# Threshold attention into a bilinear FFN: the scores of the last 64 queries on the other two 64x64 tiles of the PE array

## The chip, the cores and the metric

The kernel runs on one core of a Trainium2 chip. The metric is the device time of one execution in microseconds (us): 1541.02 us before the change, the median of three runs (1540.39 to 1543.94). Profiles are of one execution each.

## The reference, cut to what matters

There are 8 batches of 8 heads, 576 positions and head size 64, everything in fp32. The 64 heads' outputs are laid side by side per batch into 4608 rows of 512, which go through a bilinear feed-forward network (FFN) with 1536 inner columns.

```python
scores = scale * np.matmul(q, k.transpose(0, 1, 3, 2))
thresh = np.max(scores, axis=-1, keepdims=True) - tau
scores = np.where(scores >= thresh, scores, -1000000000.0)
scores = scores - np.max(scores, axis=-1, keepdims=True)
attn = np.exp(scores)
attn = attn / (np.sum(attn, axis=-1, keepdims=True) + 1e-09)
attn_out = np.matmul(attn, v)                      # (8, 8, 576, 64)
x = attn_out.transpose(0, 2, 1, 3).reshape(4608, 512)
out = (x @ w_a) * (x @ w_b) @ w_out
```

## The kernel before, in words

**Tiles of the array.** Every large product is cut to 64 contraction rows by 64 output columns, so each matmul occupies one quarter of the 128x128 PE array. Which quarter follows from the partitions: the operands' partitions (0-63 or 64-127) give the row half r, the output's partitions give the column half c. This text writes a tile as (r,c). (0,0) and (1,1) are the diagonal pair, (0,1) and (1,0) the off-diagonal pair. Both halves of a head pair lie in the two partition halves of `qT` and `kT`, so r is the head in a pair.

**Units.** The 64 heads are 32 pairs. A pair's 576 queries are five units: `u` = 0 to 3 with 128 queries each and `u` = 4 (`NT`) with the last 64 (`TAIL`). `scores` (L303 to L322) multiplies a unit's queries with all 576 keys in two halves `c` of 288. A full unit has eight matmuls, two on each tile, into two buffers of the accumulation memory (PSUM), one a head. The last unit has four, all into one buffer: head 0 into its lower 64 partitions, head 1 into its upper 64.

**After the scores.** DVE takes each row's maximum (L319), GpSimd the threshold and the bias (L320, L321), ACT the exponential (L332), DVE masks and sums (L336), ACT divides (L355). `turn_blocks` (L393 to L426) has DVE transpose 32x32 blocks into `tb` (for the last unit, `tbt`), sends them out to a scratch tensor `swap` in DRAM, from where `turn_back` fetches the transposed weights `wT` for two parts of a pair: 256 queries (units 0 and 1), and 320 (units 2, 3 and 4). For the first four pairs the parts are 256, 256 and 64 wide, and their first eight units are turned on the PE instead.

**Product with v.** `product` (L441 to L451) multiplies a part's `wT` with `v`. The 1152 keys of a pair (576 a head) are nine slots of 128 partitions: four for each head, which use all four tiles in turn, and slot `NT`, which the heads share: its lower 64 partitions hold keys of head 0 and its upper 64 keys of head 1. In that slot there are only two matmuls, (0,0) and (1,1). It comes first in the product.

**FFN.** `ffn` (L505 to L563) is a generator of small steps; each step on `pab` (L530, the products with `w_a` and `w_b`, 256 columns) and on `po` (L550, the product with `w_out`, 512 columns) issues four matmuls, in the order (0,0), (0,1), (1,0), (1,1). A block of 256 rows is 2 x 6 groups of `pab` with 8 steps, and 2 groups of `po` with 12.

**Order.** The loop from L634 writes the order of all engines' instructions out by hand, and `keep_order` keeps it. One turn `g` issues the scores of unit `g`, then FFN steps (`advance`, in portions), the weighing of unit `g`, more FFN steps, the product of a part whose last unit was four turns ago (`PV_LAG`, L675 to L679), and FFN steps. After the first four pairs, a group of four pairs takes 20 turns (L616, L617):

```python
units += [(p, u) for p in range(i, i + HP) for u in (0, 1)]
units += [(p, u) for p in range(i, i + HP) for u in (2, 3, NT)]
```

With the turns of a group counted from 0, its last units have their scores in turns 10, 13, 16 and 19, its products of 256 come in turns 5, 7, 9 and 11, and those of 320 in turns 14, 17, 20 and 23 (the last two are turns 0 and 3 of the next group).

Of the kernel before, what the change touches and what calls it, by code (L numbers as in the profile page):

```python
# [50 lines left out]
def kernel(  # L51
# [8 lines left out]
    w_out: bass.AP,  # L60
    out: bass.AP,
):

# [23 lines left out]
    B, H, S, D = q.shape  # L89
    P = 128  # L90
# [4 lines left out]
    NT = 4  # L95
    MAIN = NT * P
    TAIL = S - MAIN
    assert D == 64 and TAIL == 64 and DM == HP * P
    NB = S // Q
# [22 lines left out]
    def banks(n, name):  # L122

        return psum.tile([P, 2, 512], FP32, tag="banks", name=name)[:, :, 0:n]
# [120 lines left out]
    for _ in range(2):  # L245
        t = work.tile([P, 2 * NB, 2 * Q], FP32, tag="tb", bufs=2, name="rows")
        t = t.rearrange("p n e -> p (n e)")[0:R]
# [11 lines left out]
    for name in ("q", "k"):  # L259
        t = work.tile([P, CW, 2], FP32, tag="xT", bufs=XT_BUFS, name="rows")  # L260
        t = t.rearrange("p n e -> p (n e)")[0:R, 0:2 * NR * D]
# [41 lines left out]
    def scores(i, u):  # L303
        qT, kT = prepared[i]["q"], prepared[i]["k"]
        n = 2 if u < NT else 1
        sc = [banks(SH, "sc") for _ in range(n)]
        for c in range(2):
            for t in range(n):
                for j in range(2):
                    r = slice(j * D, (j + 1) * D)  # L310
                    q0, to = (u * P + t * D, slice(t * D, (t + 1) * D)) if u < NT else (MAIN, r)
                    nc.tensor.matmul(sc[j if u < NT else 0][to, c], qT[r, q0:q0 + D],  # L312
                                     kT[r, c * SH:(c + 1) * SH], start=True, stop=True)
        mx = small.tile([P, 2], FP32, tag="mx", name="mx")
        thr = small.tile([P, 2], FP32, tag="thr", name="thr")
        bias = small.tile([P, 2], FP32, tag="bias", name="bias")
        for j in range(n):
            c = slice(j, j + 1)
            nc.vector.tensor_reduce(mx[:, c], sc[j], axis=AX.XY, op=ALU.max)  # L319
            nc.gpsimd.tensor_scalar(bias[:, c], mx[:, c], e_nscale, None, op0=ALU.mult)  # L320
        nc.gpsimd.tensor_scalar(thr[:, 0:n], mx[:, 0:n], cut, None, op0=ALU.subtract)  # L321
        scored[i, u] = (sc, thr, bias)  # L322
# [61 lines left out]
    def part(i, u):  # L384

        if i < HP:
            return {1: (i, 0), 3: (i, 1), NT: (i, 2)}.get(u)
        return {1: (i, 0), NT: (i, 1)}.get(u)

    def width(i, h):  # L390
        return (HALF, HALF, TAIL)[h] if i < HP else (HALF, HALF + TAIL)[h]

    def turn_blocks(i, u):  # L393

        ws, _ = weights.pop((i, u))
        if u < NT:
            if u % 2 == 0:
                tbufs[i] = work.tile([P, 2 * NB, 2 * Q], FP32, tag="tb", bufs=2, name="tb")
            tb = tbufs[i]
            for j, w in enumerate(ws):  # L400
                nc.vector.transpose(  # L401
                    tb[:, j * NB:(j + 1) * NB, (u % 2) * Q:(u % 2 + 1) * Q],
                    w.rearrange("p (n e) -> p n e", e=Q))
            if u % 2 == 0:
                return
            h = u // 2
            n = width(i, h)
            swap = scratch.tile([2 * NB, Q, n], FP32, tag=f"swap{n}", name="swap")
            swaps[i, h] = swap
            for g in range(G):  # L410
                nc.sync.dma_start(  # L411
                    swap[:, :, g * 2 * Q:(g + 1) * 2 * Q].rearrange("c p w -> p c w"),
                    tb[g * Q:(g + 1) * Q])
        else:
            tb = work.tile([P, S], FP32, tag="w", bufs=W_BUFS, name="tbt").rearrange("p (n e) -> p n e", e=Q)
            nc.vector.transpose(tb.rearrange("p n e -> p (n e)"), ws[0])
            if i < HP:
                swaps[i, 2] = scratch.tile([2 * NB, Q, TAIL], FP32, tag="swapt", name="swap")
            swap = swaps[part(i, u)]
            for g in range(G):  # L420
                c = slice(g // 2 * NB, (g // 2 + 1) * NB)
                w0 = swap.shape[2] - TAIL + (g % 2) * Q
                nc.sync.dma_start(swap[c, :, w0:w0 + Q].rearrange("c p w -> p c w"),  # L423
                                  tb[g * Q:(g + 1) * Q])
        if part(i, u):
            ready.append(part(i, u))  # L426
# [207 lines left out]
    for g in range(len(units) + PV_LAG):  # L634
# [3 lines left out]
        if here:  # L638
            i, u = units[g]
            scores(i, u)  # L640
# [18 lines left out]
        if g > BY_PE and g <= len(units):  # L659
            turn_blocks(*units[g - 1])  # L660
# [86 lines left out]
```

## Time and profile before

| what | value |
|---|---|
| time | 1541.02 us (1540.39 to 1543.94) |
| PE matmuls (PE) | busy 1484.0 us, 96%, 22640 records |
| PE weight loads (PEld) | busy 1145.4 us, 74% |
| DVE / ACT / GpSimd | busy 878.4 / 590.0 / 261.6 us, 57 / 38 / 17% |
| records of the scores (L312) | 2304 |
| records of the product with v (L449) | 2592 |
| DMA queue q1 | 64.1% of sixteen engines' span |

The kernel's code has 1152 score matmuls (128 full units of eight, 32 last units of four); the profile has 2304 records on their line, two for each. So one fp32 matmul is two passes of its tile, each with its own weight load and record. Records of the same pass on different tiles overlap, and the busy time of a row counts overlapped time once: a row's busy time says little about how many of the four tiles ran. A record's length is modelled, and longer than the tile is occupied. The spacing of the starts on one tile tells that.

### The profile page before, as it was taken

What the parts mean: (1) busy time and instruction counts of PE and PEld (TensorE: products, weight loads), DVE (VectorE), ACT (ScalarE), POOL (GpSimd) and SP (SyncE); (2) the same over time, 40 slices, a digit from 0 to 9 for tenths busy, and PEclk for the clock granted to TensorE, in tenths of its full rate; (3) what the DMA queues carried; (4) which work ended last, traced back from release to release, by engine and by line L of the source; (5) the groups of instructions that cost most, each with busy time, mean ns of one, the idle gap of its engine ahead of it and who ended that gap; (6) DMA issues with size and microseconds to landing.
All of it is one profiled execution on the core that took longest, in us unless ns stands there. A gap on an engine that the chain in (4) does not pass through costs nothing.

```text
span 1541.0 us, 51117 instructions
## 1 busy us (share of the span) xinstructions
PE 1484.0 (96%) x22640; PEld 1145.4 (74%) x22640; DVE 878.4 (57%) x1844; ACT 590.0 (38%) x935; POOL 261.6 (17%) x662
## 2 busy tenths in 40 slices
PE   5778999999999999999999999999999999999998
PEld 3666786675777576778777787877777879798886
DVE  5999676567656765665545754576645665510010
ACT  4767354334433443443323433344433443410000
POOL 2666211101110111020100101011110111110000
PEclk8889999999999999999999999999999999999999
DMA  9658888679868876795547966588748876430000
GB/s 202 150 139 226 173 174 194 163 152 188 192 148 155 185 182 150 147 193 133 123 100 145 190 149 138 119 173 177 171 95 159 182 173 125 123 84 15 2 15 15
DMA packets 624557, 220.38 MB, mean 143 GB/s; under 512 B 542928, under 2 KB 612048, under 8 KB 624336
## 3 DMA queue, kind: packets, MB, share of 16 engines
q1 hardware_dynamic: 621968, 216.52, 64.1%
q8 instruction: 178, 2.92, 0.8%
q10 hardware_dynamic: 2368, 0.59, 0.2%
q14 instruction: 43, 0.35, 0.1%
HBM read 127.40 MB, written 89.65 MB: 141 GB/s over the span
## 4 chain that ended last, share of the span: by engine, by line
PE 88%; DVE 5%; SPq 2%; ACT 1%; issue 1%; DMA 1%; POOL 0%; POOLq 0%; DVEq 0%; ACTq 0%
PE pab L530 45%; PE po L550 24%; PE pv L449 9%; PE sc L312 9%; DVE low L226 1%; SPq L140 1%; DVE w L336 1%; DVE mx L319 1%; SPq L411 1%; DMA raw<-in_moe_w_b_dram 0%; PE tp L374 0%; DVE tb L401 0%; SPq L423 0%; DVE wb_sb L232 0%; DVE wo_sb L232 0%
## 5 line engine op out<-in xcount | busy, mean ns | idle before, releaser
L550 PE MATMUL po<-wo_sb,h 64*64 64x512 f32 x3456 | 424.3, 589 | 0.0
L550 PEld LDWEIGHTS po<-wo_sb,h 64*64 64x64 f32 x3456 | 222.8, 133 | 137.6 <-issue 79.7
L319 DVE TENSOR_REDUCE mx<-sc 128x1 f32<-128x576 f32 x288 | 205.0, 748 | 201.4 <-PE sc L312 201.2
L332 ACT ACTIVATE w<-sc,bias,scalars 128x576 f32<-128x576 f32 x288 | 226.8, 827 | 190.2 <-POOL bias L320 178.7
L312 PE MATMUL sc<-kT,qT 64*64 64x288 f32 x2304 | 264.1, 412 | 21.5 <-DVE w L336 9.8
L530 PE MATMUL pab<-xS,wa_sb 64*64 64x256 f32 (+1 forms) x3520 | 278.7, 376 | 3.3 <-POOL xS L459 3.3
L530 PE MATMUL pab<-xS,wb_sb 64*64 64x256 f32 (+1 forms) x3520 | 279.4, 377 | 2.5 <-issue 2.5
L355 ACT ACTIVATE w<-w,rcp 128x576 f32<-128x576 f32 x272 | 197.7, 768 | 182.9 <-DVE rcp L349 182.7
L320 POOL TENSOR_SCALAR bias<-mx,scalars 128x1 f32<-128x1 f32 x288 | 85.5, 297 | 1050.3 <-DVE mx L319 624.5
L530 PE MATMUL pab<-xT,wb_sb 64*64 64x256 f32 (+1 forms) x3136 | 250.9, 377 | 0.5 <-DVE h L538 0.5
L530 PE MATMUL pab<-xT,wa_sb 64*64 64x256 f32 (+1 forms) x3136 | 243.4, 373 | 4.4 <-DVE xT L439 3.5
L336 DVE SCALAR_TENSOR_TENSOR w<-sc,thr,w 128x576 f32<-128x576 f32 x288 | 222.4, 804 | 20.5 <-ACT w L332 17.8
L530 PEld LDWEIGHTS pab<-xS,wa_sb 64*64 64x64 f32 x3520 | 193.4, 134 | 33.6 <-POOL xS L459 9.8
L530 PEld LDWEIGHTS pab<-xS,wb_sb 64*64 64x64 f32 x3520 | 196.5, 135 | 27.9 <-issue 3.1
L312 PEld LDWEIGHTS sc<-kT,qT 64*64 64x64 f32 x2304 | 148.2, 134 | 71.6 <-issue 18.3
L530 PEld LDWEIGHTS pab<-xT,wa_sb 64*64 64x64 f32 x3136 | 170.4, 133 | 30.4 <-DVE xT L439 3.8
L530 PEld LDWEIGHTS pab<-xT,wb_sb 64*64 64x64 f32 x3136 | 173.5, 135 | 24.4 <-DVE h L538 1.1
L449 PE MATMUL pv<-wT,vm 64*64 64x320 f32 (+3 forms) x2592 | 186.1, 382 | 1.9 <-ACT h L536 1.4
L401 DVE STREAM_TRANSPOSE tb<-w 128x576 f32<-128x576 f32 x240 | 171.3, 752 | 1.3 <-ACT w L355 1.3
L449 PEld LDWEIGHTS pv<-wT,vm 64*64 64x64 f32 x2592 | 138.8, 134 | 37.3 <-issue 7.4
L538 DVE TENSOR_TENSOR h<-h,pab 128x512 f32<-128x512 f32 (+1 forms) x110 | 72.8, 662 | 125.3 <-PE pab L530 124.8
L536 ACT COPY h<-pab 128x512 f32<-128x512 f32 (+1 forms) x110 | 63.2, 574 | 203.9 <-PE pab L530 203.1
(59 smaller groups left out, 747.9 us busy)
## 6 DMA issues: line engine op xcount, KB each, us to landing
swap<-tb SPq DMA_DIRECT2D x240, 288.0 KB, 5.3
wT<-swap SPq DMA_DIRECT2D x28, 1440.0 KB, 7.4
wT<-swap SPq DMA_DIRECT2D x32, 1152.0 KB, 6.4
vm<-in_v_dram SPq DMA_DIRECT2D x32, 288.0 KB, 4.5
swap<-tbt SPq DMA_DIRECT2D x128, 72.0 KB, 2.6
out_dram<-osb SPq DMA_DIRECT2D x32, 256.0 KB, 4.0
qm<-in_q_dram SPq DMA_DIRECT2D x112, 72.0 KB, 3.5
km<-in_k_dram SPq DMA_DIRECT2D x112, 72.0 KB, 4.4
```

The costliest lines, as they stand in the source:

```text
L312: nc.tensor.matmul(sc[j if u < NT else 0][to, c], qT[r, q0:q0 + D], kT[r, c * SH:(c + 1) * SH], start=True, stop=True)
L319: nc.vector.tensor_reduce(mx[:, c], sc[j], axis=AX.XY, op=ALU.max)
L320: nc.gpsimd.tensor_scalar(bias[:, c], mx[:, c], e_nscale, None, op0=ALU.mult)
L332: nc.scalar.activation(w.rearrange("p (c k) -> p c k", c=2), s, AF.Exp, bias=bias[:, j:j + 1], scale=e_scale)
L336: nc.vector.scalar_tensor_tensor(out=wv, in0=s, scalar=thr[:, j:j + 1], in1=wv, op0=ALU.is_ge, op1=ALU.mult, accum_out=sums[:, j:j + 1])
L355: nc.scalar.activation(w, w, AF.Copy, scale=rcp[:, j:j + 1])
L401: nc.vector.transpose(tb[:, j * NB:(j + 1) * NB, (u % 2) * Q:(u % 2 + 1) * Q], w.rearrange("p (n e) -> p n e", e=Q))
L449: nc.tensor.matmul(pv[j * D:(j + 1) * D, r], vm[rows, k0], wT[rows, k0], start=(s == (NT if j == r else 0)), stop=(s == NT - 1))
L530: nc.tensor.matmul(pab[c * D:(c + 1) * D, r], w[rows, f // n, k, fs + c * D:fs + (c + 1) * D], moving, start=(k == 0), stop=(k == H - 1))
L536: nc.scalar.copy(ht, pab)
L538: nc.vector.tensor_tensor(ht, ht, pab, op=ALU.mult)
L550: nc.tensor.matmul(po[c * D:(c + 1) * D, r], ht[rows, t0:t0 + D], wo_sb[rows, F, :], start=(F == 0), stop=(F == NF - 1))
```

## The change

In the last unit, head j's scores go to the other half of the partitions: head 0 (row half 0) into partitions 64-127, head 1 (row half 1) into 0-63. That moves these four matmuls from the diagonal pair of tiles, which the shared slot of the product with v also uses, to the off-diagonal pair. All row-wise work after it is the same on swapped partitions; where the transposed blocks are written out, the block range `c` of each group of 32 partitions is swapped back, so `swap` holds the same data as before. For full units (`u < NT`) the new expressions give the old values.

```diff
             for t in range(n):
                 for j in range(2):
                     r = slice(j * D, (j + 1) * D)
-                    q0, to = (u * P + t * D, slice(t * D, (t + 1) * D)) if u < NT else (MAIN, r)
+                    o = t if u < NT else 1 - j
+                    q0, to = (u * P + t * D if u < NT else MAIN), slice(o * D, (o + 1) * D)
                     nc.tensor.matmul(sc[j if u < NT else 0][to, c], qT[r, q0:q0 + D],
                                      kT[r, c * SH:(c + 1) * SH], start=True, stop=True)
...
             swap = swaps[part(i, u)]
             for g in range(G):
-                c = slice(g // 2 * NB, (g // 2 + 1) * NB)
+                c = slice((1 - g // 2) * NB, (2 - g // 2) * NB)
                 w0 = swap.shape[2] - TAIL + (g % 2) * Q
                 nc.sync.dma_start(swap[c, :, w0:w0 + Q].rearrange("c p w -> p c w"),
                                   tb[g * Q:(g + 1) * Q])
```

## The prediction

> **What bounds the kernel now.** I read the page first: the engines' shares, then the chain that ended last.
>
> ```profile
> PE 1484.0 (96%) x22640; PEld 1145.4 (74%) x22640; DVE 878.4 (57%) x1844; ACT 590.0 (38%) x935; POOL 261.6 (17%) x662
> ...
> PE 88%; DVE 5%; SPq 2%; ACT 1%; issue 1%; DMA 1%; POOL 0%; POOLq 0%; DVEq 0%; ACTq 0%
> ```
>
> The PE is the bound: 96% busy, 88% of the chain. Next, stretches, and the waits of the PE after 230 us:
>
> ```profile
> 0.00:230.00 230.00, 185.94 (x2931) 147.67 (x2935) 181.47 (x341) 130.00 (x236) 105.31 (x160) 0.93 0.79 178
> 230.00:1345.00 1115.00, 1107.36 (x16788) 835.11 (x16784) 675.12 (x1468) 443.12 (x670) 149.40 (x485) 1.00 0.72 156
> ...
> PE pab L530 <- issue: 2.5, 1, 2.5
> PE pab L530 <- POOL xS L459: 2.4, 2, 1.4
> PE pv L449 <- ACT h L536: 1.4, 2, 0.7
> PE sc L312 <- DVE sums L347: 1.3, 2, 0.9
> ```
>
> (The first number after each stretch is its length, the second PE busy.) From 230 to 1345 us, where 28 of the 32 last units lie, the PE stands still for only 7.6 us, at full clock. So the question is not whether the PE waits but whether all four tiles run. That is in the PE's timeline around one last unit's scores, at 1291 us, and in that of the weight loads:
>
> ```profile
> 1290.42 1.18 PE L530 MATMUL pab<-xT,wa_sb 64*64 64x256 f32 x12
> 1291.28 0.89 PE L312 MATMUL sc<-kT,qT 64*64 64x288 f32 x5
> 1291.77 0.43 PE L530 MATMUL pab<-xT,wa_sb 64*64 64x256 f32 x2
> 1291.92 0.49 PE L312 MATMUL sc<-kT,qT 64*64 64x288 f32 x2
> 1292.04 0.38 PE L530 MATMUL pab<-xT,wa_sb 64*64 64x256 f32 x2
> 1292.17 0.40 PE L312 MATMUL sc<-kT,qT 64*64 64x288 f32 x1
> ...
> 1292.74 0.38 PE L530 MATMUL pab<-xS,wa_sb 64*64 64x256 f32 x2
> ...
> 1293.11 1.67 PE L530 MATMUL pab<-xS,wa_sb 64*64 64x256 f32 x25
> ...
> 1291.07 0.83 PEld L312 LDWEIGHTS sc<-kT,qT 64*64 64x64 f32 x7
> 1291.77 0.20 PEld L530 LDWEIGHTS pab<-xT,wa_sb 64*64 64x64 f32 x4
> 1291.93 0.13 PEld L312 LDWEIGHTS sc<-kT,qT 64*64 64x64 f32 x1
> ```
>
> First, the pace. From 1293.11 to 1294.84 (where the next group of 32 records takes over) the FFN starts 32 records on four tiles in 1.73 us, so a tile starts one 256-column pass each 216 ns, 0.844 ns a column. A pass of 288 columns is then 243 ns, of 320 columns 270 ns. Second, the last unit: its eight score passes, four on each diagonal tile, hold those tiles from 1291.28 to 1292.25, 4 x 243 = 972 ns. In the 16 pass slots of 1290.42 to 1291.28 and the 16 of the next 0.97 us there are only 12 + 12 records. The eight missing are the off-diagonal tiles, idle for four slots each, 0.86 us. Third, how far tiles drift apart: the FFN's records of 1292.04 start before the last score pass of 1292.17, so the tiles don't run in lockstep. But they don't run freely: the off-diagonal tiles got their next weights at 1291.77, just as the seventh of eight score loads was done, that is, when (0,0) had loaded its last pass. [...] In the steady FFN the off-diagonal pair passes from xT to xS at 1292.74 and (0,0) at 1293.11: a lead of 0.37 us. [...]
>
> So the diagonal pair is the bound. Everything else is spread evenly over four tiles, but the shared slot and the last unit's scores both come on top of it, while the off-diagonal pair waits at the end of its lead.
>
> [...]
>
> **The change, part by part.**
> - The four score matmuls stay four, with the same operands and columns. What changes is who pays: 4 x 243 = 0.972 us off each diagonal tile for each of 32 pairs, 31.1 us, and on to each off-diagonal tile.
> - The shared slot stays on the diagonal: two passes of 256 (0.432) and two of 320 (0.540), again 0.972 us a pair. Afterwards both tile pairs have equal work. 31.1 us is the ceiling of the gain.
> - The maximum, exponential, mask, transpose and the four transfers (tbt to swap, 72 KB, 2.6 us) are as many and as large: nothing, on engines of 57% and less and a queue at 64%. No wait is added; the product needs the transfers four turns later.
>
> How much of the ceiling is kept depends on how far each pair may run ahead. Let x be the off-diagonal lead over (0,0). Scores of a last unit take 0.972 off x, a product adds 0.432 or 0.540. What would push x past its upper end, +0.375, is lost by the off-diagonal pair; past its lower end it is lost by the diagonal pair, which is time of the kernel. The lower end no trace of before shows, since the diagonal pair never leads. [...] Bounds: -0.375 and -0.807. I take -0.807, [...].
>
> One group of four pairs, in the order of turns. The products of turns 0, 3, 5, 7 and 9 have x at +0.375. Turn 10 scores: -0.597, nothing lost. Turn 11 product: -0.165. Turn 13 scores: -1.137, so 0.330 lost, x = -0.807. Turn 14 product: -0.267. Turn 16 scores: 0.432 lost. Turn 17 product, turn 19 scores: 0.432 lost. Then five products in a row bring x back to +0.375 and waste the rest. Kept: 4 x 0.972 - 1.194 = 2.694 us a group, in seven groups 18.9 us. With -0.375 the losses are 0.222 + 0.540 + 0.432 + 0.432 and 7 x 2.262 = 15.8 us stay. The first four pairs have scores at 162, 168, 175 and 182 us and only one product between, at 173: losses of 0.762, 0.540 and 0.972 leave 1.6 us, of which I count half, 0.8, because the PE also waits there (46.64 us busy of 150 to 200). I take off 1 us for (1,1)'s falling behind, once at 0.4 and again after some of the waits that bring the tiles level. Sum: 18.9 + 0.8 - 1.0 = 18.7, so 1541.0 - 18.7 = 1522.
>
> **Rivals.**
> - *Nearly all is kept:* [...] the 512-column po passes, whose products last 864 ns, hold more lead. Against it: the 0.37 us seen in the other direction. 31.1 less about 1: 1511 us.
> - *The diagonal pair can't lead at all,* [...]. For it: it never does so now. Each last unit then uses up the off-diagonal lead only, 28 x 0.375 = 10.5: 1530.5 us.
> - *Nothing:* the diagonal pair is stopped wherever scores run beside it. Against it: the off-diagonal FFN ran beside diagonal scores now. 1541 us.
> - *Slower:* the last matmul of a group is on (1,1), on which its reader waits. With (1,0) behind, the group must be waited for to its end; [...]. Against it: four buffers in turn, and PE waits of 7.6 us in 1115.
>
> **How the numbers follow.** My forecast, with both lower ends: 0.64 (1522 likeliest, 1525 at -0.375). Nearly all: 0.13. No lead: 0.12. Nothing: 0.06. Slower: 0.05. The range 1510 to 1532 takes in the first three. Faster: 0.64 + 0.13 + 0.12 = 0.89; same 0.06; slower 0.05.
>
> **What the profile after would show.** The score records of a last unit run between FFN records of the diagonal pair with no slots missing (about 16 records in 0.97 us at turn 10). Right after, the diagonal pair passes from group to group ahead of the other, by up to 0.8 us. In turns 16 and 19 diagonal slots are missing. The stretch 230 to 1345 shortens by about 18 us, the one after it by nothing. I am wrong if the diagonal tiles pause at each last unit, if waits of pab on DVE or ACT appear, or if the DMA queue, 79% in 230 to 560 us, takes over.

## The result, and the profile after

The changed kernel takes 1525.81 us (median; 1524.84 to 1528.06) against 1541.45 us before on the same chip (the median of four runs, the three from above and one more): a ratio of 0.9898, 95% interval 0.9881 to 0.9915, 15.6 us less. Two repeats below gave 1524.52 and 1523.55 us. The prediction was 1522, and faster.

The page of the changed kernel, shares of the engines and the chain that ended last:

```profile
PE 1467.9 (96%) x22640; PEld 1145.1 (75%) x22640; DVE 877.9 (58%) x1844; ACT 588.9 (39%) x935; POOL 260.4 (17%) x662
...
PE 87%; DVE 6%; DMA 3%; SPq 1%; ACT 1%; issue 1%; POOL 0%; DVEq 0%; ACTq 0%; POOLq 0%
```

As many records as before, the PE still 96% busy, and 16.1 us less of it: the same passes lie closer together. What the PE waited for after 230 us (its waits, us in total, times, longest) stayed small, 6.3 us where it was 7.6:

```profile
PE pab L533 <- POOL xS L462: 2.4, 2, 1.4
PE pv L452 <- ACT h L539: 1.4, 2, 0.7
PE sc L315 <- DVE sums L350: 1.3, 2, 0.9
PE pv L452 <- DMA wT<-swap: 0.7, 1, 0.7
PE pab L533 <- issue: 0.5, 1, 0.5
```

The line with `wT` is new: once, at 249 us, the PE waits 0.7 us for a transfer of transposed weights, though the prediction had no wait added. One repeat (e2) has this wait with 0.5 us, another (e11) not at all.

The gain is in the PE's timeline. These are the scores of a last unit in turn 10 (pair 28), right after a product; lines are three further down than before (L312 is now L315, L449 L452, L530 L533):

```profile
1250.06 1.62 PE L452 MATMUL pv<-wT,vm 64*64 64x256 f32 x24
1251.36 0.41 PE L315 MATMUL sc<-kT,qT 64*64 64x288 f32 x2
1251.46 0.43 PE L452 MATMUL pv<-wT,vm 64*64 64x256 f32 x2
1251.60 0.41 PE L315 MATMUL sc<-kT,qT 64*64 64x288 f32 x2
1251.67 0.38 PE L452 MATMUL pv<-wT,vm 64*64 64x256 f32 x1
1251.73 0.38 PE L533 MATMUL pab<-xS,wa_sb 64*64 64x256 f32 x1
1251.84 0.41 PE L315 MATMUL sc<-kT,qT 64*64 64x288 f32 x2
1251.89 0.43 PE L533 MATMUL pab<-xS,wa_sb 64*64 64x256 f32 x2
1252.09 0.41 PE L315 MATMUL sc<-kT,qT 64*64 64x288 f32 x2
1252.12 1.67 PE L533 MATMUL pab<-xS,wa_sb 64*64 64x256 f32 x24
```

The score passes start in twos, one on each off-diagonal tile, 243 ns apart (1251.36, .60, .84, 1252.09), and between them the diagonal tiles go on with the product and the FFN. In these four slots (1251.36 to 1252.33) 16 passes start, as the prediction said, where the kernel before had 12. Of these scores only the output's partitions were changed, and with them the slots in which their passes run. Then who is ahead, three turns later (pair 29):

```profile
1278.62 0.38 PE L533 MATMUL pab<-xT,wb_sb 64*64 64x256 f32 x1
1278.76 0.44 PE L533 MATMUL pab<-xS,wa_sb 64*64 64x256 f32 x3
1278.84 0.38 PE L533 MATMUL pab<-xT,wb_sb 64*64 64x256 f32 x1
1278.98 0.38 PE L533 MATMUL pab<-xS,wa_sb 64*64 64x256 f32 x2
1279.05 0.38 PE L533 MATMUL pab<-xT,wb_sb 64*64 64x256 f32 x2
1279.19 0.38 PE L533 MATMUL pab<-xS,wa_sb 64*64 64x256 f32 x2
1279.26 1.46 PE L533 MATMUL pab<-xT,wb_sb 64*64 64x256 f32 x21
```

One tile, (0,0), passes to the next FFN group at 1278.62. The off-diagonal pair starts its last two passes of the old one at 1279.19 and so changes 216 ns later, at 1279.41: it is now 0.79 us behind. Before, it was 0.37 ahead.

The kernel's code gives the order in which each tile gets its matmuls, and the passes of one tile follow each other at 216, 243, 269 or 429 ns (256, 288, 320 and 512 columns; the records themselves mostly last 376, 402, 429 and 589 ns). So the records can be sorted to their tiles, and x, the lead of (0,1) over (0,0), read at any FFN step as the difference of two starts. One group of four pairs (20 to 23), in us, with x as it stands after each step, once it has settled (within four FFN steps):

```
turn, what           before    changed   saved since turn 10   the prediction's x
10  scores           +0.43     -0.65     0.97                  -0.60
11  product 256      +0.32     -0.21     0.97                  -0.17
13  scores           +0.32     -0.79     1.54                  -0.81
14  product 320      +0.32     -0.25     1.54                  -0.27
16  scores           +0.32     -0.79     2.08                  -0.81
17  product 320      +0.42     -0.25     2.08                  -0.27
19  scores           +0.43     -0.85     2.68                  -0.81
```

(Saved: how much earlier (0,0) starts the same FFN step than before.) The prediction had 2.694 us for a group. From just before turn 10 to after turn 19 (0,0) gains 2.62 to 2.68 us in each of the six groups from pair 8 on, read in `pab` steps, and e2 and e11 below, the same kernel again, have the same to 0.01 us.

### The profile page after: what moved, and what is told of

Read it like the earlier page. It is cut to its first block, busy times and chain, and to the rows that moved or that the text cites. A ratio compares the mean times of both kernels' runs of the same rounds, so it can differ in the third digit from the quotient of the medians.

```text
span 1524.0 us, 51117 instructions
## 1 busy us (share of the span) xinstructions
PE 1467.9 (96%) x22640; PEld 1145.1 (75%) x22640; DVE 877.9 (58%) x1844; ACT 588.9 (39%) x935; POOL 260.4 (17%) x662
## 4 chain that ended last, share of the span: by engine, by line
PE 87%; DVE 6%; DMA 3%; SPq 1%; ACT 1%; issue 1%; POOL 0%; DVEq 0%; ACTq 0%; POOLq 0%
PE pab L533 45%; PE po L553 23%; PE pv L452 9%; PE sc L315 9%; DVE low L228 2%; DMA raw<-in_moe_w_a_dram 1%; DVE w L339 1%; DVE mx L322 1%; DVE tb L404 1%; DMA wT<-swap 0%; SPq L414 0%; SPq L426 0%; DVE wa_sb L234 0%; SPq L142 0%; DMA swap<-tb 0%
## 5 line engine op out<-in xcount | busy, mean ns | idle before, releaser
L553 PEld LDWEIGHTS po<-wo_sb,h 64*64 64x64 f32 x3456 | 226.0, 133 | 130.3 <-issue 73.4
L533 PE MATMUL pab<-xS,wa_sb 64*64 64x256 f32 (+1 forms) x3520 | 278.6, 373 | 3.3 <-POOL xS L462 3.3
L533 PE MATMUL pab<-xS,wb_sb 64*64 64x256 f32 (+1 forms) x3520 | 278.2, 375 | 0.5 <-issue 0.5
L315 PE MATMUL sc<-kT,qT 64*64 64x288 f32 x2304 | 254.4, 417 | 19.7 <-DVE w L339 8.4
L533 PE MATMUL pab<-xT,wb_sb 64*64 64x256 f32 (+1 forms) x3136 | 249.0, 374 | 1.7 <-DVE h L541 1.7
L533 PE MATMUL pab<-xT,wa_sb 64*64 64x256 f32 (+1 forms) x3136 | 246.2, 375 | 3.0 <-DVE xT L442 1.8
L533 PEld LDWEIGHTS pab<-xS,wa_sb 64*64 64x64 f32 x3520 | 193.5, 133 | 35.5 <-POOL xS L462 10.1
L533 PEld LDWEIGHTS pab<-xS,wb_sb 64*64 64x64 f32 x3520 | 197.0, 134 | 27.6 <-issue 1.1
L533 PEld LDWEIGHTS pab<-xT,wa_sb 64*64 64x64 f32 x3136 | 175.2, 134 | 28.9 <-DVE xT L442 2.1
L315 PEld LDWEIGHTS sc<-kT,qT 64*64 64x64 f32 x2304 | 148.0, 136 | 63.0 <-issue 20.1
L452 PE MATMUL pv<-wT,vm 64*64 64x320 f32 (+3 forms) x2592 | 192.8, 384 | 2.3 <-ACT h L539 1.4
L533 PEld LDWEIGHTS pab<-xT,wb_sb 64*64 64x64 f32 x3136 | 176.1, 134 | 24.2 <-DVE h L541 2.3
L452 PEld LDWEIGHTS pv<-wT,vm 64*64 64x64 f32 x2592 | 149.2, 137 | 28.8 <-issue 8.1
```

What stands on the lines that cost most here:

```text
L452: nc.tensor.matmul(pv[j * D:(j + 1) * D, r], vm[rows, k0], wT[rows, k0], start=(s == (NT if j == r else 0)), stop=(s == NT - 1))
L533: nc.tensor.matmul(pab[c * D:(c + 1) * D, r], w[rows, f // n, k, fs + c * D:fs + (c + 1) * D], moving, start=(k == 0), stop=(k == H - 1))
L553: nc.tensor.matmul(po[c * D:(c + 1) * D, r], ht[rows, t0:t0 + D], wo_sb[rows, F, :], start=(F == 0), stop=(F == NF - 1))
```

## The experiments

Theory: the tiles drift apart only as far as the order of issue lets them, between -0.81 us (an end that no trace had shown, the author's estimate) and +0.375 (+0.37 in the trace before), and what a moved last unit saves depends on where x stands, so on the order of scores and products. Rivals: a share that is the same for each moved unit; ends that belong to the tiles; a gain that is independent of the order. Each run is beside runs of the kernel before on its chip.

**e1 and e2, both kernels again**, no edit. The first profile of the changed kernel was 3.4 us behind before any changed instruction had run.

> The kernel before once more, word for word but for a comment. Theory (start-up scatter): in the profile of the changed kernel the first 162 us, before any changed instruction, were 3.4 us longer than before; if that is scatter between runs, the same code shows such a difference again: unit (0, 4) at 162 us plus or minus 3, total 1541 within 3. Rival (the change itself slows the start): this run has its last units' scores of the first four pairs begin at 162.0 within 0.3.

> The changed kernel once more. Theory: 1526 within 3; from the first scores of pair 7 (about 235 us) to the end it gains 19 to 20 us on the kernel before, as in the first profile, because leads of the tiles follow the order of issue and not the run; the start differs by up to 3 us either way. Rival (the change slows the start): unit (0, 4) begins at 165.4 again, within 0.3.

Measured: e1 1543.8 us (ratio 1.0008, 0.9998 to 1.0017), unit (0, 4) at 162.75 us. e2 1524.52 us (0.9882, 0.9866 to 0.9899), unit (0, 4) at 162.73, not at 165.4. From the first scores of pair 7 to the PE's last start it takes 1280.5 us, the first profile 1281.4, the kernel before 1300.7 and e1 1300.0: 19 to 20 less. About 2 us of this are not the work of the tiles: at one step of the FFN in pair 29 the PE stands still without a releaser that the profile shows, for 2.5 us in the kernel before and 1.9 in e1, for 0.5 in the first profile of the changed kernel and not at all in e2. Without this gap the stretch is 17 to 18 us shorter. So the change doesn't have to slow the start; the same code has both starts, and e11 below has the late one again.

**e3, half of the last units moved** (pairs 0 and 2 of each four; where the blocks are written out, the range follows, as it does in e7):

```diff
-                    o = t if u < NT else 1 - j
+                    o = t if u < NT else (1 - j if i % 2 == 0 else j)
```

> Only the last units of pairs 0 and 2 of each four are moved to the off-diagonal tiles (in turns 10 and 16), those of pairs 1 and 3 stay on the diagonal. Theory (leads with ends at -0.81 and +0.375 us): each moved unit finds the off-diagonal pair at its upper end and saves its whole 0.972 us, 2 x 7 x 0.972 = 13.6 us in the seven later groups of pairs against 18.9 with all moved, so about 1531. Rival (each moved unit saves its average share): half of 18.9, 9.5 us, so about 1534.

Measured: 1530.25 us (0.9914, 0.9897 to 0.9930), 12.3 us under the 1542.52 beside it; 12.2 in the trace from pair 7 on (1288.5 against 1300.7). Half of the moves keep well over half of the gain. The rival's 9.5 is out: moved units don't bring equal shares. The trace says it group by group: (0,0) gains 1.94 us in five of the six groups from pair 8 on and 1.88 in the other, twice 0.97, where equal shares would be 1.35.

**e7, only the last of four moved** (turn 19):

```diff
-                    o = t if u < NT else 1 - j
+                    o = t if u < NT else (1 - j if i % 4 == 3 else j)
```

> Only the last unit of every fourth pair (turn 19) is moved to the off-diagonal tiles. Theory (leads with ends): alone it finds the off-diagonal pair at its upper end and saves all of its 0.972 us, 7 x 0.972 = 6.8 us and about 0.5 in the first four pairs, so about 1535; with all four moved the same one saved only 0.54. Rival (a share for each): a quarter of 18.9, 4.7, so 1537.5; or 7 x 0.54 = 3.8, so 1538.5.

Measured: 1537.05 us (0.9957, 0.9933 to 0.9981), 6.1 less than 1543.16; the interval of the ratio, 2.9 to 10.3 us, can't exclude the rivals. The trace can: from pair 7 on it is 8.9 us under the kernel before (1291.8), of which 2.5 us are the gap in pair 29, at 1204 us, which e7 doesn't have. The remaining 6.4 is nearer to 6.8 than to 4.7 or 3.8. And in each of the six groups from pair 8 on (0,0) gains 0.97 us, the whole of the theory's 0.972; the rivals are 0.67 and 0.54 a group. The same unit saved 0.54 us when all four were moved.

**e8, the FFN's order of issue turned round**, off-diagonal tiles first (the same for `po`):

```diff
-                    for r in range(2):
-                        ...
-                        for c in range(2):
+                    for r, c in ((0, 1), (1, 0), (0, 0), (1, 1)):
```

> The changed kernel with the FFN's four matmuls of a step issued in the order (0,1), (1,0), (0,0), (1,1) instead of (0,0), (0,1), (1,0), (1,1). Theory (the ends of the lead come from the order of issue): the ends change sides; the off-diagonal pair now leads (0,0) by up to 0.81 us and (0,0) leads by 0.375 at most; the room between them is as large, so the time stays, 1525 within 2. Rival (the ends belong to the tiles): leads as in the changed kernel, -0.79 to +0.375.

Measured: 1523.04 us (0.9876, 0.9861 to 0.9891). The lower end moved as said, the upper didn't: in FFN steps after 380 us x stays between -0.37 and +0.37 in most and never passes +0.48. A miss by half: x rises in the product, and there (0,0) still came first. The room between the ends was therefore not as large as before, and (0,0) gains 2.25 us in each of the six groups instead of 2.62 to 2.68. That is the prediction's own walk with ends at -0.375 and +0.375, which keeps 2.262. The time of the whole kernel, within the range expected, doesn't show these 2.5 us over six groups.

**e9, the same order in the product's full slots and in full units' scores too:**

```diff
-            for r in range(2):
-                ...
-                for j in ((r,) if s == NT else range(2)):
+            for r, j in ((0, 0), (1, 1)) if s == NT else ((0, 1), (1, 0), (0, 0), (1, 1)):
```

> As e8, and the full units' scores and the product's four full slots too are issued in the order (0,1), (1,0), (0,0), (1,1). In e8 the lower end moved to -0.37 as the theory says, but x rose to 0.37 to 0.48 only, and in the product, where the extra diagonal work comes, the order was still the old one. Theory (ends come from the order of issue, where the lead is made): now x rises to 0.7 or more after the products in a row (turns 20, 23, 5, 7, 9) and stays between -0.37 and 0.81; the time is that of the changed kernel, 1524 within 2. Rival (the upper end of 0.375 belongs to the off-diagonal tiles): x stays under 0.5, and the losses of a lower end of -0.37 remain.

Measured: 1521.22 us (0.9852, 0.9840 to 0.9865), 0.8 us below the range expected. The PE's timeline after a row of products:

```profile
898.81 0.38 PE L530 MATMUL pab<-xS,wb_sb 64*64 64x256 f32 x2
...
899.39 0.38 PE L530 MATMUL pab<-xT,wb_sb 64*64 64x256 f32 x2
899.46 1.40 PE L530 MATMUL pab<-xS,wb_sb 64*64 64x256 f32 x20
900.54 0.59 PE L549 MATMUL po<-wo_sb,h 64*64 64x512 f32 x2
900.69 0.60 PE L530 MATMUL pab<-xS,wb_sb 64*64 64x256 f32 x4
...
901.34 0.66 PE L549 MATMUL po<-wo_sb,h 64*64 64x512 f32 x4
```

Two tiles pass to the next FFN group at 898.81 and to `po` at 900.54, the other two follow at 899.61 (216 ns after the last pair of old passes) and 901.34: the off-diagonal pair is 0.80 us ahead, where it never was over 0.48 with the diagonal first. In the same group of pairs as above:

```
turn, what           changed   e8        e9
before turn 10       +0.32     +0.37     +0.80
10  scores           -0.65     -0.42     -0.17
11  product 256      -0.21     +0.06     +0.26
13  scores           -0.79     -0.37     -0.37
14  product 320      -0.25     +0.17     +0.17
16  scores           -0.79     -0.37     -0.37
17  product 320      -0.25     +0.17     +0.17
19  scores           -0.85     -0.42     -0.42
```

The ends are those of the order of issue, mirrored with it: -0.79 and +0.37 became -0.37 and +0.80. That rules out ends that belong to the tiles. With the room restored, (0,0) gains 2.67 or 2.68 us in five of the six groups and 2.55 in the last: as much as in the changed kernel, as the theory has it, and not more.

**e4, products of 256 later**, so that after each last unit one or two products follow and nothing should be lost at the lower end:

```diff
+LATE = (6, 5, 6, 7)
+    def lag(i, u):
+        return PV_LAG + (LATE[i % HP] if i >= HP and u == 1 else 0)
...
-            n = g - PV_LAG
-            if BY_PE <= n < len(units) and part(*units[n]):
+            for n in [n for n in range(BY_PE, len(units)) if part(*units[n]) and n + lag(*units[n]) == g]:
```

The edit also gives the scratch tensor `swap` eight buffers and starts the transfers of `wT` two turns before their product, so later.

> The changed kernel with the products of 256 queries issued later: not in turns 5, 7, 9 and 11 but 11, 12, 15 and 18, so that every last unit (10, 13, 16, 19) is followed by one or two products (11 and 12, 14 and 15, 17 and 18, 20 and 23). Theory (leads with ends): after each last unit x = -0.6 to -0.7, and the products bring it back to +0.27 or more, nothing is lost: 28 x 0.972 = 27.2 us instead of 18.9, 8.3 us faster than the changed kernel, about 1517.5. Rival (the gain doesn't depend on the order): as the changed kernel, 1526.

Measured: 1535.86 us (0.9947, 0.9933 to 0.9962), a miss by 18. One stretch of the changed kernel, 165 to 330 us (its length, then the busy time of PE, weight loads, DVE, ACT and GpSimd), and the same of e4:

```profile
165.00:330.00 165.00, 161.70 (x2557) 122.76 (x2555) 108.09 (x238) 71.77 (x109) 24.89 (x79) 1.00 0.80 172
```

```profile
165.00:330.00 165.00, 150.97 (x2191) 100.75 (x2186) 118.81 (x262) 75.47 (x116) 26.94 (x87) 0.97 0.86 188
```

The later products finish the FFN's rows of the first groups later: there were 442 fewer `pab` passes in this stretch (987, where the changed kernel has 1429), and the PE ran 10.7 us less. Its waits there sum to 13.8 us, where the changed kernel has 3.3; 3.8 of them are for transfers of `wT`, the rest for DVE, ACT and GpSimd. That too little FFN work was left to fill the turns fits this, and e5, but what the later transfers cost was not separated from it. But in pairs 16 to 27, where the FFN has work in store, (0,0) stood idle for 0.6 us in all; in the changed kernel it is 4.5. The tiles did as the theory says; the schedule took more than they gave.

**e5 and e6: late products from pair 16 on only**, with the new place of the scores and with the old one:

```diff
-        return PV_LAG + (LATE[i % HP] if i >= HP and u == 1 else 0)
+        return PV_LAG + (LATE[i % HP] if i >= 4 * HP and u == 1 else 0)
```

> The changed kernel with the late products (turns 11, 12, 15, 18 instead of 5, 7, 9, 11) only from pair 16 on, where there is FFN work in store to fill the turns that lose a product. Theory (leads with ends, and e4 lost at the start because the FFN ran dry, not because of the array): in the four groups from pair 16 on nothing is lost at the lower end, 4 x 1.194 = 4.8 us faster than the changed kernel, about 1520; diagonal tiles idle there under 0.5 us a group instead of 1.1 to 2.0. Rival (late products cost time wherever they are): 1526 or more.

> The order of e5 with the scores of the last 64 queries left on the diagonal tiles as before. Theory: the diagonal pair is never without work, so the order can't matter: 1542, as before. Rival (the late products themselves save or cost): off from 1542 by more than 2.

Measured: e5 1522.06 us (0.9870, 0.9853 to 0.9888). e6 1543.83 us (1.0005, 0.9993 to 1.0016): on the old place the later products show no change in the time, as the theory has it.

**e10 and e11: e5 and the changed kernel on one chip.**

> e5 once more, beside the changed kernel on one chip, to see whether the late products from pair 16 on are faster than it. Theory: by 3 to 5 us, 1520 to 1522. Rival (what the array gains, the turns without a product lose): the same as e11 within 1.

> The changed kernel once more, beside e10: 1525 within 2. Its first last unit's scores (0, 4) between 162 and 166 us, the stretch from the first scores of pair 7 to the end 1281 within 1.

Measured: e10 1521.03 us (0.9857, 0.9843 to 0.9872), e11 1523.55 us (0.9879, 0.9858 to 0.9900), with unit (0, 4) at 166.0 and 1283.2 us from pair 7 on, 2 more than expected; beside e2, 0.5 us of it are the gap in pair 29, and the rest is lost before the last unit of pair 8. e10 is 2.5 us faster by the medians, but the intervals overlap. Of the 4.8 us hoped for, (0,0)'s idle time in pairs 20 to 31 gives back 2.3 (2.3 us, where e11 has 4.6), and pairs 16 to 19 give nothing (2.2, where e11 has 1.9): not the under 0.5 us a group that e5 was to show. The PE's waits from 640 to 1310 us, of e10, have a new line:

```profile
PE pv L458 <- issue: 1.6, 3, 0.7
```

It stands still before some of the late products, for which the profile shows no releaser. What that is stays open.

**e12: e9's order with e5's late products.**

> Order of issue of e9 and late products from pair 16 on as in e5. Theory: in the last four groups x goes 0.80, -0.17, +0.69, -0.28 and so on between the ends, nothing is lost there, so 2 to 3 us under e9's 1521: about 1519. Rival (the late products gain nothing beside e9): 1521 to 1522.

Measured: 1521.07 us (0.9859, 0.9840 to 0.9879). No gain beside e9 shows in the time; the interval is too wide to exclude 2 us, but from pair 7 on e12 takes 1278.5 us and e9 1279.3. e9, e10 and e12 are the fastest of all, 1521 us; by their medians 2.3 to 2.5 us under e11, with intervals that overlap.

## Why the prediction was right

**The bound.** It named the diagonal pair of tiles, on eight missing pass slots. Right: in the trace before, (0,0) is idle for about 11 us and (0,1) for about 65 from pair 7 on; in the changed kernel both for about 18 (spacing of the starts less the length of a pass, good to 2 us). The 28 last units are 28 x 0.972 = 27.2 us less for (0,0), of which 7.7 came back as idle time, 19.5 stay, the gap in pair 29 included.

**How far the tiles drift.** This was the step without a trace to show it: -0.375 and -0.807 as lower ends were the author's estimates, and -0.807 was taken. Measured -0.79. (1,1) was 0.4 to 0.5 us behind (0,0) when x settled at that end; in the group shown it was 0.48 behind before the change too. That the order of issue sets the ends is shown by e8 and e9: with the off-diagonal tiles first they were -0.37 and +0.80 instead of -0.79 and +0.37.

In the weight loads of before, 1291.77 is the start of the seventh score load, not its end. What the records show of the ends is this: where x reaches one, it stands right after a last unit at +0.48 (before the change) or -0.96 (after it), nearly one or two matmuls of 2 x 243 ns, and the next `pab` steps bring it in by about 0.05 us each, to +0.37 or +0.32, or to -0.79. A tile that had stood idle took 267 ns from its first pass to its second (1291.77 to 1292.04), 51 more than the 216; whether that makes the steps of 0.05 is not shown. So the end of -0.807 came out right in size; why it lies there and not further out is not shown.

**The walk through the turns.** 2.694 us a group was predicted, 2.62 to 2.68 measured in six of seven. Pairs 4 to 7 gave 2.3, and 1.1 in e11. In the first profile the PE waits 0.9 us between the first two of their last units (at 284 us, for `xS`), and before them 0.7 us for `wT` (the new wait at 249 us); what each of the two took from the gain was not separated. The logic of the walk, that a unit's worth depends on x, is shown by the gains a group of e3 (1.94), e7 (0.97) and e8 (2.25).

**The rest of the sum.** The first profile has 19.6 us from 231 us to 1355, of which 1.8 belongs to the gap in pair 29, which was shorter than before. The 17.8 left is what the sum has for the groups after its 1 us off, 17.9. That they agree so closely is in part luck: the 1 us was taken off for (1,1)'s falling behind, and no group from pair 8 on loses as much as 0.1 to it; up to 1 us was lost or won between the groups instead, and in pairs 4 to 7. The first profile also has 1.1 us in the first four pairs, where 0.8 was put, and 3.4 us lost before 162 us, a term that the sum didn't have; with 0.3 lost at the end it is 17.0 in all. The part between the first scores of pair 7 and the last of all went from 1108.5 to 1089.7 us, the part after it from 192.2 to 191.7: 18.8, or 17 without the gap, and nothing, where about 18 and nothing was said. By the medians of three comparisons the gain is 15.6, 18.0 and 19.9 us. So the first result is the low one of three and the sum was right in size; the missing term is the start. Why it comes late in some runs is open. The three profiles with the scores on the old place all began at 162 to 163 us; of the eleven others seven did, and four at 165 to 166. Three are too few to tell whether the change has a part in it.

**The rivals.** A diagonal pair that can't lead, 1530.5, is refuted by x = -0.79. "Nothing" and "slower" needed PE pauses or waits; those of the PE after 230 us went down from 7.6 to 6.3 (2.0 less in the gap of pair 29, 0.7 more for `wT`). "Nearly all is kept" failed on the order of turns: e4 kept nearly all in pairs 16 to 27, where scores and products alternate.

## What to carry to other kernels

Add up the passes of each quarter of the PE array and not of the PE: here a PE that was 96% busy had two quarters with about 65 us of idle time, and the two fuller ones, with about 11, set the time. Moving the uneven work to the other quarters paid even where it didn't lie next to what it balanced, as long as the imbalance stayed within the leads measured here (0.79 us for the diagonal pair, 0.37 for the other); after that the gain depended on how the two kinds of work alternate. In this kernel each moved unit was worth 0.97 us alone and 0.67 us on average with the other three of its group. Before reordering for the sake of the array, look at what else the order feeds: in e4 the FFN came late, and 11 us of what the move had won were lost.

## What the runs showed that had not been expected

- The lead that one pair of tiles has survived many FFN steps and a change of their shape: after the last unit of pair 20 x stood at -0.65 for 12 us, and after the next product at -0.21 for 9 us, until the next last unit. The tiles came nearly level after a wait of the PE (0.9 us before the scores at 504.6 us in the changed kernel: x from -0.26 to +0.01), and also without one that the profile lists, in the scores of a full unit at 1184.9 us (x from -0.26 to -0.07).
- The pair of the tile issued first was the one that came to be 0.80 us ahead (0.79 on the diagonal), the other came to 0.37; and it counted where the lead is made. With the new order in the FFN alone (e8) the upper end stayed at 0.48, with it in the product too (e9) it was 0.80.
- Right after the scores of a last unit the diagonal lead was up to 0.96 us (once 1.23). `pab` steps cut it back to 0.79 within four steps; in `po` steps, with 512 columns a pass, it stayed at 0.85 or 0.91 until the next `pab` steps.
